# Rescheduling the combine weights of the second mixture, and the place of the low parts in an expert's first unit

## The chip, the cores and the metric

The kernel runs on one core of one Trainium2 chip. The metric is the device time of one execution in microseconds, the median of several runs; lower is better. A core has five engines with a queue of instructions each: TensorE (PE, matrix products), VectorE (DVE), ScalarE (ACT), GpSimd (POOL) and SyncE (SP, which here only issues DMA transfers). An engine works its queue in order, and an instruction waits on semaphores that other engines or transfers raise.

## The reference

Attention with a memory, then a soft mixture of experts, then a second mixture whose gates are balanced over rows and columns. The change touches the second mixture alone:

```python
def _moe_ref(x, phi, w1, w2):            # first mixture; its output is the second one's x
    ...
    return (c @ slot_out).astype(np.float32)      # c: 2304 x 32, slot_out: 32 x 512

def _moe2_ref(x, w_gate, w1, w2):
    N, D = x.shape                        # 2304, 512
    E = w_gate.shape[1]                   # 8 experts
    P = np.exp(logits - logits.max())     # logits = x @ w_gate
    for _ in range(8):
        P /= P.sum(1, keepdims=True) + 1e-09
        P /= P.sum(0, keepdims=True) + 1e-09
        P *= N / E
    for e in range(E):
        h = np.maximum(x @ w1[e], 0.0)    # 2304 x 1024
        ye = h @ w2[e]                    # 2304 x 512
        out += P[:, e:e + 1] * ye
```

## The kernel before, in words

Since x is `c @ slot_out`, with 32 slots, the first layer of expert e is `c @ (slot_out @ w1[e])`. The small product in brackets is formed by `prepare_a`, split by `split_a`, and copied into its place by 16 transfers (`move_a`, line 1077; sources `ahi` and `alo`). The weights c are multiplied by the gate P[:, e] beforehand, which is allowed because P is positive. So each expert needs its own turned combine weights: the tile `c4T`, whose 128 rows are four stacked copies of 32 slots, two of high parts and two of low parts (a float32 is split into a rounded part "h" and the rest "l", so that fast products keep the accuracy).

The 2304 tokens are nine units of 256. The 72 units (eight experts, nine units) run one after the other; a unit g has seven steps, k = 0 to 6. In step k TensorE makes one of seven products of the second layer (`product`, a scheme with seven instead of eight block products; the order is p5, p1, p7, p6, p2, p3, p4). Each product has 4 blocks f with three terms: high by high, high by low part of the weights (`wl`), low part of h by high: 12 matmuls with 256 columns. In step 1 TensorE also makes the first layer of the next unit (`layer1`, line 1097, 8 matmuls), so a unit has 92 matmuls. A unit of the first expert up to unit 4 is done in plain form (`plain`).

The weights of an expert are prepared during the units of the expert before: sums (line 996), high parts on ACT (line 999), low parts on POOL or DVE (line 1005). Those of the tiles BB1 and BB2 (named B11, T3, B21, B22 in the code) are overwritten in place, and their turn comes only in the last unit and the first one of the next expert, since the last unit still reads them.

The new combine weights for c4T come in two rounds, r = 0 for token tiles 0 to 8 and r = 1 for tiles 9 to 17: `part_c` (POOL: c by P[:, e]), `round_c` (ACT: high part), `rest_c` (POOL: low part), `blocks_c` twice (DVE: 32 by 32 blocks turned, z = 0 the high part, z = 1 the low part, into a tile `ct` of which there is one buffer), and `move_c` (SP: 16 transfers of 36 KB into c4T, line 1333). Before the change both rounds belong to units 5 and 6 of the expert before, and their transfers follow in units 5 and 7.

The order on PE, DVE, ACT and POOL is the order in which the loop at the end writes the instructions (`manual_schedule`); a table `side` says after which step the functions above are called: `beside(s, f)` puts f after step s = 7 g + k, `at(u, k, f)` is the same with unit and step apart. SP's order comes from the framework's scheduler and is shown below. With v = 9 (e - 1), units v to v + 8 are those of expert e - 1, and v + 9 is the first of expert e.

Of the kernel before, what the change touches and what calls it, by code (L numbers as in the profile page):

```python
# [21 lines left out]
def infini_attention_soft_moe_sinkhorn_moe(  # L22
# [15 lines left out]
    nc = tc.nc  # L38
    B, H, D, S = q.shape
# [72 lines left out]
    with ExitStack() as actx:  # L112
# [31 lines left out]
        for i in range(QTB):  # L144
            pr = []
            for nm, w in (("qz", 3 * TAIL), ("qx", 2 * TAIL)):
                t = e2.tile([P, w], F32R, name=f"{nm}{i}")
# [5 lines left out]
        for i in range(2):  # L153
            t = ep[i].tile([P, 2, S], F32R, name=f"klz{i}")
# [530 lines left out]
        def at(p, n, f, *args):  # L685

            fill.setdefault(3 * NT * p + n, []).append((f, args))
# [14 lines left out]
        for p in range(NP):  # L702
            b, hp = order[p]
# [68 lines left out]
    with bctx:  # L772
# [7 lines left out]
        for i in range(NBIG + 4, len(pieces)):  # L780

            k = i % (NBIG + 4 + NW)
# [140 lines left out]
    KH = KF // 2  # L923
# [401 lines left out]
            ct_[e, r, "t"][:, WR * z : WR * z + WR], cw[:, WR * (1 - z) : WR * (2 - z)]  # L1325
        )

    def move_c(e, r):
        ct = ct_[e, r, "t"]
        to = c4T[:, 0:N].bitcast(F32).rearrange("p (t j n) -> p t j n", j=4, n=32)  # L1330
        for z in range(4):
            for j in range(4):
                nc.sync.dma_start(  # L1333
                    to[32 * z : 32 * z + 32, NR * r : NR * r + NR, j],
                    ct[32 * j : 32 * j + 32, WR * (z // 2) : WR * (z // 2) + WR].rearrange(
                        "p (t n) -> p t n", n=32
                    ),
                )
# [3 lines left out]
    def beside(s, f, *args):  # L1342
        side.setdefault(s, []).append((f, args))
# [22 lines left out]
    def at(u, k, f, *args):  # L1366
        beside(7 * u + k, f, *args)

    def c_round(v, e, r, w):
        at(v, 1, part_c, e, r)  # L1370
        at(v, 2, round_c, e, r)
        at(v, 3, rest_c, e, r)
        at(v, 4, blocks_c, e, r, 0)
        at(v, 5, blocks_c, e, r, 1)
        at(w, 6, move_c, e, r)

    for k, u0, u1 in ((-1, 5, 7), (2, 7, 9)):
        for n, f in enumerate((scale_c, turn_c, store_c)):
# [1 line left out]
    s = 1  # L1380
# [9 lines left out]
        at(RAW - 1, 5 + i, w_lo, 0, "T3", i, "P")  # L1390
    for e in range(1, E):
        v = NU * (e - 1)
        c_round(v + 5, e, 0, v + 5)
        c_round(v + 6, e, 1, v + 7)
        at(v, 0, load_w1, e, e % 2)
        at(v + 3 * (e == 1), 4, load_raw, e)

        at(v + 1, 3 + 2 * (e == 1), prepare_a, e)
        at(v + 1, 4 + (e == 1), split_a, e)
        at(v + 1, 5 + (e == 1), move_a, e)  # L1400
        for i in range(2):
            for n, nm in enumerate(("T1", "T2", "T4")):

                s = 29 + 4 * (3 * i + n) if e == 1 else 7 * (v + 2 + 3 * i + n) + 1
                beside(s, w_sum, e, nm, i, "P")
                beside(s + 2 - (e == 1), w_hi, e, nm, i)
                beside(s + 3 - (e == 1), w_lo, e, nm, i, "P")
            at(v + 6 + i, 2, w_sum, e, "T3", i, "P")
        for nm, k in (("B11", 2), ("T3", 4), ("B21", 6), ("B22", 8)):
            for i in range(2):  # L1410
                at(v + 8, k + i, w_hi, e, nm, i)
                at(v + 8, k + i + (nm[0] == "B" and nm[1] == "2"), w_lo, e, nm, i, "D" if nm == "B22" and i else "P")
# [30 lines left out]
    def product(g, k):  # L1443
        e, u = units[g]
        a, b = PRODS[ORDER[k]]
        bank, half = PLACE[ORDER[k]]
        if (g, bank) not in Y:
            Y[g, bank] = ps_y.tile([P, DM], F32, tag="y", name=bank)
        o_ = Y[g, bank][:, CW * half : CW * half + CW]
        hh, hl = X[g, a, "h"], X[g, a, "l"]  # L1450
        wh, wl = W[e, b, "h"], W[e, b, "l"]
        for f in range(KH):
            nc.tensor.matmul(o_, hh[:, f, :], wh[:, f, :], start=f == 0, stop=False)  # L1453
            nc.tensor.matmul(o_, hh[:, f, :], wl[:, f, :], start=False, stop=False)  # L1454
            nc.tensor.matmul(o_, hl[:, f, :], wh[:, f, :], start=False, stop=f == KH - 1)  # L1455
        return o_

    def collect(g, k, y):
# [68 lines left out]
    with tc.manual_schedule(engines={E_.PE, E_.DVE, E_.Activation, E_.Pool}):  # L1527
# [27 lines left out]
        for g in range(len(units)):  # L1555
            nxt = g + 1 < len(units)
            for k in range(7):
                s = 7 * g + k
# [16 lines left out]
                else:  # L1575

                    EX[s + 1] = g, k, product(g, k)
                    if k == 1 and nxt:
                        layer1(g + 1)
# [74 lines left out]
```

## Time and profile before

| what | value |
|---|---|
| median of 3 runs (range) | 1141.69 us (1140.42 to 1143.72) |
| the profiled execution | 1150.51 us |
| its span in the trace, granted TensorE clock | 1148.4 us, 0.984 of full speed |
| busy: PE, DVE, POOL, ACT | 1091.0, 824.8, 680.7, 614.8 us |
| transfers into c4T (line 1333) | 224, 36 KB each, 2.0 us to landing |

The profiled execution is 8.8 us longer than the median of the plain runs. All times of single instructions below come from that execution. The second mixture begins at about 311 us, and its experts run from about 382 us to the end. "Busy" counts the time in which an engine works on at least one instruction; matmuls overlap, so a matmul that lasts 0.28 us in a row is followed by the next some 0.11 to 0.12 us after its own start.

### The profile page before, as it was taken

The page shows a single profiled execution, that of the slowest core. Times are in us where ns is not written, and L with a number is a line of the kernel's source. Part 1 is how long each engine was busy: PE and PEld are TensorE (multiplying, and loading weights), DVE is VectorE, ACT ScalarE, POOL GpSimd, SP SyncE. Part 2 cuts the span into 40 slices and gives each one's busy share as a digit, 9 for nine tenths or more (in the row PEclk, how much of TensorE's full clock was granted, in tenths as well). Part 3 has the DMA queues.
Part 4 walks back from the last instruction along what each step waited for, and adds up shares of the span by engine and source line. Part 5 has one row for each costly group of instructions (what it writes and reads, how often), then busy time and mean ns, then how long its engine had stood idle before and what let it go on. Part 6 is the DMA issues. An engine that isn't in the chain of part 4 may idle for free.

```text
span 1148.4 us, 24415 instructions
## 1 busy us (share of the span) xinstructions
PE 1091.0 (95%) x9103; PEld 990.2 (86%) x9103; DVE 824.8 (72%) x1839; ACT 614.8 (54%) x1301; POOL 680.7 (59%) x633
## 2 busy tenths in 40 slices
PE   6989998998999999999999999999999999999998
PEld 4767777773377899999899999999999999999998
DVE  7878888875167457777777777777777777777775
ACT  6788878761242656446344544544454454445442
POOL 4423333300153598688578767867776776788665
PEclk9999999997999999999999999999999999999999
DMA  6577677428922024014102501420150132011111
GB/s 152 161 219 223 193 217 219 106 105 354 383 88 74 1 41 149 19 22 132 57 1 32 158 19 20 119 71 1 30 160 19 17 97 92 5 27 24 54 51 55
DMA packets 110740, 113.97 MB, mean 99 GB/s; under 512 B 76320, under 2 KB 86688, under 8 KB 106528
## 3 DMA queue, kind: packets, MB, share of 16 engines
q1 hardware_dynamic: 110192, 112.34, 33.1%
q8 instruction: 72, 1.18, 0.4%
q14 instruction: 44, 0.36, 0.1%
q10 hardware_dynamic: 432, 0.09, 0.0%
HBM read 95.74 MB, written 4.72 MB: 87 GB/s over the span
## 4 chain that ended last, share of the span: by engine, by line
PE 67%; DVE 10%; POOL 5%; SPq 5%; ACT 5%; issue 4%; DMA 3%; DVEq 0%; ACTq 0%; POOLq 0%
PE y L1454 15%; PE y L1453 15%; PE y L1455 15%; PE l L1097 5%; SPq L1333 4%; PE po L447 3%; PE y L1420 3%; POOL BB2l L1005 2%; DMA kd<-in_k_dram 2%; PE pt L410 1%; PE ph L841 1%; DMA c4T<-ct 1%; PE pso L863 1%; ACT sm L371 1%; PE pa L1044 1%
## 5 line engine op out<-in xcount | busy, mean ns | idle before, releaser
L1121 DVE SCALAR_TENSOR_TENSOR f<-l,f 128x512 f32<-128x512 f32 x268 | 184.3, 688 | 89.5 <-ACT a11h L1127 70.8
L1138 POOL TENSOR_TENSOR s1l<-f,s1h 128x512 fp32r<-128x512 f32 x67 | 87.0, 1299 | 137.2 <-ACT s1h L1127 137.1
L1469 DVE TENSOR_TENSOR accA<-accA,y 128x512 f32<-128x512 f32 x125 | 85.5, 684 | 55.0 <-PE y L1455 54.0
L1117 ACT ACTIVATE f<-l 128x512 f32<-128x512 f32 x67 | 40.2, 599 | 138.7 <-PE l L1097 112.0
L1127 ACT ACTIVATE a12h<-l 128x512 fp32r<-128x512 f32 x72 | 43.2, 600 | 128.4 <-PE y L1455 88.0
L1138 POOL TENSOR_TENSOR s4l<-f,s4h 128x512 fp32r<-128x512 f32 x67 | 87.1, 1300 | 26.9 <-ACT s4h L1127 23.0
L1469 DVE TENSOR_TENSOR accB<-accB,y 128x512 f32<-128x512 f32 x125 | 85.1, 681 | 8.0
L1138 POOL TENSOR_TENSOR s3l<-f,s3h 128x512 fp32r<-128x512 f32 x67 | 87.0, 1298 | 2.0 <-ACT s3h L1127 2.0
L1138 POOL TENSOR_TENSOR s2l<-f,s2h 128x512 fp32r<-128x512 f32 x67 | 86.9, 1297 | 0.0
L1097 PE MATMUL l<-c4T,a 128*128 128x256 f32 x576 | 79.9, 282 | 4.3 <-DVE a22l L1134 4.3
L1454 PE MATMUL y<-BB2l,s4h 128*128 128x256 f32 x268 | 76.1, 284 | 6.4 <-POOL BB2l L1005 4.3
L1453 PE MATMUL y<-T1h,s1h 128*128 128x256 f32 x268 | 75.3, 281 | 4.8 <-DVE accA L1469 4.7
L371 ACT ACTIVATE sm<-sm,mn 128x128 f32<-128x128 f32 (+3 forms) x128 | 71.0, 556 | 15.9 <-DVE mn L367 14.6
L1005 POOL TENSOR_TENSOR BB1l<-raw,BB1h 128x512 fp32r<-128x512 f32 x32 | 41.5, 1311 | 62.6 <-ACT BB1h L999 62.6
L1097 PEld LDWEIGHTS l<-c4T,a 128*128 128x128 f32 x576 | 72.8, 189 | 6.1 <-DVE a22l L1134 5.7
L1454 PE MATMUL y<-BB2l,a12h 128*128 128x256 f32 x268 | 75.5, 282 | 0.3
L1453 PE MATMUL y<-BB2h,s4h 128*128 128x256 f32 x268 | 75.1, 280 | 0.7 <-ACT accD L1467 0.7
L1453 PE MATMUL y<-BB2h,a12h 128*128 128x256 f32 x268 | 75.5, 282 | 0.0
L1453 PE MATMUL y<-BB1h,a11h 128*128 128x256 f32 x268 | 75.3, 281 | 0.0
L1453 PE MATMUL y<-BB1h,s3h 128*128 128x256 f32 x268 | 75.3, 281 | 0.0
L1454 PE MATMUL y<-BB1l,s3h 128*128 128x256 f32 x268 | 75.3, 281 | 0.0
L1454 PE MATMUL y<-T4l,a22h 128*128 128x256 f32 x268 | 75.3, 281 | 0.0
(321 smaller groups left out, 4137.8 us busy)
## 6 DMA issues: line engine op xcount, KB each, us to landing
wm<-in_moe_w_dram SPq DMA_DIRECT2D x32, 1024.0 KB, 8.5
raw<-in_moe_w_dram SPq DMA_DIRECT2D x32, 512.0 KB, 4.4
w<-in_moe_w_dram SPq DMA_DIRECT2D x32, 512.0 KB, 5.1
qd<-in_q_dram SPq DMA_DIRECT2D x30, 288.0 KB, 4.2
kd<-in_k_dram SPq DMA_DIRECT2D x30, 288.0 KB, 4.7
c4T<-ct SPq DMA_DIRECT2D x224, 36.0 KB, 2.0
qp<-in_q_dram SPq DMA_DIRECT2D x15, 288.0 KB, 3.1
vt<-in_v_dram SPq DMA_DIRECT2D x16, 256.0 KB, 2.7
```

The lines of the kernel that those rows point to most:

```text
L371: nc.scalar.activation(out=sm[:, 0:n], in_=sm[:, 0:n], func=AF.Exp, scale=-1.0, bias=mnc, accum_out=X.sums[:, i, h : h + 1],)
L1005: eng(g).tensor_tensor(out=w_tile(e, nm, "l")[:, h], in0=full(e, nm, i), in1=w_tile(e, nm, "h")[:, h].bitcast(F32), op=ALU.subtract,)
L1097: nc.tensor.matmul(ph[:, f, :], a4s[e][:, P * (KH * j + f) : P * (KH * j + f) + P], c4T[:, UT * u : UT * u + UT], start=True, stop=True,)
L1117: nc.scalar.activation(out=f_tile(g, nm), in_=ph(g, nm), func=AF.Relu)
L1121: nc.vector.scalar_tensor_tensor(out=f_tile(g, nm), in0=ph(g, src), scalar=0.0, in1=b, op0=ALU.max, op1=op)
L1127: nc.scalar.activation(out=h_tile(g, nm, "h"), in_=ph(g, nm) if a else FU[g, nm], func=AF.Relu if a else AF.Copy)
L1138: nc.gpsimd.tensor_tensor(out=lo, in0=FU[g, nm], in1=hi, op=ALU.subtract)
L1333: nc.sync.dma_start(to[32 * z : 32 * z + 32, NR * r : NR * r + NR, j], ct[32 * j : 32 * j + 32, WR * (z // 2) : WR * (z // 2) + WR].rearrange(
L1453: nc.tensor.matmul(o_, hh[:, f, :], wh[:, f, :], start=f == 0, stop=False)
L1454: nc.tensor.matmul(o_, hh[:, f, :], wl[:, f, :], start=False, stop=False)
L1455: nc.tensor.matmul(o_, hl[:, f, :], wh[:, f, :], start=False, stop=f == KH - 1)
L1469: nc.vector.tensor_tensor(out=acc, in0=acc, in1=y, op=ALU.add)
```

## The change

Two edits.

First, `c_round` gets new places. Round 0 of expert e now starts after step 2 of the fifth unit (unit 4) of expert e - 1 (one unit later for e = 1), and round 1 only after step 1 of unit 1 of expert e itself. Inside a round the high part is turned right after it is made, and its 8 transfers (z = 0, 1) are issued two steps before the low part is made; the 8 transfers of the low part (z = 2, 3) follow four steps after the first 8. Tiles 9 to 17 of c4T, which round 1 writes, are first read by the first layer of unit 4, which is made in step 1 of unit 3.

Second, in the first unit of each expert but the first, the products with the weights B11, T3, B21 and B22 make their 4 terms with the low part of the weights last instead of in every block.

```diff
-    def move_c(e, r):
+    def move_c(e, r, zs):
...
-        for z in range(4):
+        for z in zs:
...
-    def c_round(v, e, r, w):
-        at(v, 1, part_c, e, r)
-        at(v, 2, round_c, e, r)
-        at(v, 3, rest_c, e, r)
-        at(v, 4, blocks_c, e, r, 0)
-        at(v, 5, blocks_c, e, r, 1)
-        at(w, 6, move_c, e, r)
+    def c_round(s, e, r):
+        for k, f, *a in (
+            (0, part_c), (1, round_c), (2, blocks_c, 0), (5, rest_c), (6, blocks_c, 1),
+        ):
+            beside(s + k, f, e, r, *a)
+        beside(s + 3, move_c, e, r, (0, 1))
+        beside(s + 7, move_c, e, r, (2, 3))
...
-        c_round(v + 5, e, 0, v + 5)
-        c_round(v + 6, e, 1, v + 7)
+        c_round(7 * (v + 4 + (e == 1)) + 2, e, 0)
+        c_round(7 * (v + 10) + 1, e, 1)
...
-        for f in range(KH):
-            nc.tensor.matmul(o_, hh[:, f, :], wh[:, f, :], start=f == 0, stop=False)
-            nc.tensor.matmul(o_, hh[:, f, :], wl[:, f, :], start=False, stop=False)
-            nc.tensor.matmul(o_, hl[:, f, :], wh[:, f, :], start=False, stop=f == KH - 1)
+        terms = ((hh, wh), (hh, wl), (hl, wh))
+        seq = [(f, t) for f in range(KH) for t in terms]
+        if u == 0 and e and (b[0] == "B" or b == "T3"):
+            seq = [(f, t) for f in range(KH) for t in terms[::2]] + [(f, terms[1]) for f in range(KH)]
+        for n, (f, (a, b)) in enumerate(seq):
+            nc.tensor.matmul(o_, a[:, f, :], b[:, f, :], start=n == 0, stop=n == 3 * KH - 1)
```

SP's queue from the loads of expert 7's weights (`raw`, written in the first unit of expert 6) to the transfers behind `move_a` (`a`), before:

```order
L955 DMA raw_12910<-in_moe_w_dram 128x1024
L955 DMA raw_12912<-in_moe_w_dram 128x1024
L955 DMA raw_12914<-in_moe_w_dram 128x1024
L955 DMA raw_12916<-in_moe_w_dram 128x1024
L1077 DMA a_13082<-ahi 32x256 x4
L1077 DMA a_13082<-alo 32x256 x4
L1077 DMA a_13082<-ahi 32x256 x4
L1077 DMA a_13082<-alo 32x256 x4
L1333 DMA c4T<-ct 32x9x32 x32
```

The same place of SP's queue now:

```order
L955 DMA raw_12887<-in_moe_w_dram 128x1024
L955 DMA raw_12889<-in_moe_w_dram 128x1024
L955 DMA raw_12891<-in_moe_w_dram 128x1024
L955 DMA raw_12893<-in_moe_w_dram 128x1024
L1333 DMA c4T<-ct 32x9x32 x8
L1077 DMA a_13072<-ahi 32x256 x4
L1077 DMA a_13072<-alo 32x256 x4
L1077 DMA a_13072<-ahi 32x256 x4
L1077 DMA a_13072<-alo 32x256 x4
L1333 DMA c4T<-ct 32x9x32 x24
```

The 32 transfers that stood behind `move_a` were both rounds of expert 7. Now the first half of expert 6's round 1 stands ahead of `move_a`'s 16, and its second half behind them, followed by the 16 of expert 7's round 0.

DVE's queue in unit 6 of expert 6, where both halves of round 1 (`ct`) stood among the sums (`accA`, `accB`) that free the product banks `y`, before:

```order
L1134 SCALAR_TENSOR_TENSOR a11l<-l_13791,a11h 128x512
L1324 STREAM_TRANSPOSE ct<-cw 128x288
L1469 TENSOR_TENSOR accA<-accA,y_13822 128x512
L1121 SCALAR_TENSOR_TENSOR f<-l_13786,f 128x512
L1324 STREAM_TRANSPOSE ct<-cw 128x288
L1469 TENSOR_TENSOR accB<-accB,y_13800 128x512
```

The first half of expert 6's round 1 now, in unit 1 of that expert (`alo` is the split behind `prepare_a`):

```order
L1471 TENSOR_TENSOR accD<-accD,y_12980 128x256
L1324 STREAM_TRANSPOSE ct<-cw 128x288
L1121 SCALAR_TENSOR_TENSOR f<-l_12967,f 128x512
L1134 SCALAR_TENSOR_TENSOR a11l<-l_12972,a11h 128x512
L1055 TENSOR_TENSOR alo<-pa,ahi 128x256
L1471 TENSOR_TENSOR accA<-accA,y_13001 128x512
```

The transposes left unit 6's chain of sums; the first of them now runs before `alo`, so its transfers come ahead of `move_a`.

PE's queue in the first unit of expert 7 at the change from product p2 (`a12`) to p3 (`s4`), before:

```order
L1454 MATMUL y_14292<-BB2l,a12h 128x256
L1455 MATMUL y_14292<-BB2h,a12l 128x256
L1453 MATMUL y_14270<-BB2h,s4h 128x256
L1454 MATMUL y_14270<-BB2l,s4h 128x256
L1455 MATMUL y_14270<-BB2h,s4l 128x256
```

The end of p3 there now:

```order
L1457 MATMUL y_14247<-BB2h,s4h 128x256
L1457 MATMUL y_14247<-BB2h,s4l 128x256
L1457 MATMUL y_14247<-BB2l,s4h 128x256 x4
L1457 MATMUL y_14330<-T4h,a22h 128x256
L1457 MATMUL y_14330<-T4l,a22h 128x256
```

The low part BB2l was first read by the second matmul of the product, and is now first read by the ninth.

## Rows read from the trace of the kernel before

**Rows 1.** The page, parts 1 and 4: busy shares, and the chain by engine.
```profile
PE 1091.0 (95%) x9103; PEld 990.2 (86%) x9103; DVE 824.8 (72%) x1839; ACT 614.8 (54%) x1301; POOL 680.7 (59%) x633
PE 67%; DVE 10%; POOL 5%; SPq 5%; ACT 5%; issue 4%; DMA 3%; DVEq 0%; ACTq 0%; POOLq 0%
```
**Rows 2.** Waits of PE, whole span: total us, times, longest.
```profile
PE y L1453 <- DVE accA L1469: 4.7, 5, 1.4
PE y L1454 <- POOL BB2l L1005: 4.3, 6, 0.7
PE l L1097 <- DVE a22l L1134: 4.3, 7, 2.1
PE y L1454 <- DVE BB2l L1005: 2.0, 1, 2.0
```
**Rows 3.** Waits of all engines, whole span: DVE's on the transfers.
```profile
DVE ct L1324 <- DMA c4T<-ct: 17.8, 7, 3.5
```
**Rows 4.** Chain of waits in time: start us, us, what; layer1 and prepare_a.
```profile
456.10 1.86 PE pa L1044 x32
464.98 0.91 PE l L1097 x8
475.41 0.91 PE l L1097 x8
...
893.54 0.94 PE l L1097 x8
...
904.38 0.94 PE l L1097 x8
...
928.11 1.20 PE l L1097 x8
938.83 0.91 PE l L1097 x8
...
961.03 0.91 PE l L1097 x8
964.66 1.86 PE pa L1044 x32
...
984.63 0.94 PE l L1097 x8
```
**Rows 5.** Timeline of PE, 905 to 956: matmuls after a wait (in brackets).
```profile
924.63 0.36 PE L1453 MATMUL y<-T1h,s1h 128*128 128x256 f32 x1 [1.41 <-DVE accA L1469]
...
928.11 1.20 PE L1097 MATMUL l<-c4T,a 128*128 128x256 f32 x8 [0.36 <-DVE a22l L1134]
...
955.41 0.39 PE L1454 MATMUL y<-BB2l,s4h 128*128 128x256 f32 x1 [0.71 <-POOL BB2l L1005]
```
**Rows 6.** Chain of waits, 860 to 965: first and last of 16 transfers.
```profile
909.58 0.63 SPq L1333
...
919.47 3.65 DMA c4T<-ct
923.44 0.48 DVE ct L1324
```
**Rows 7.** Timeline of SP, 940 to 1045: first and last quarter of move_a.
```profile
967.00 2.47 SPq L1077 DMA_DIRECT2D a<-ahi  x4
...
974.59 2.49 SPq L1077 DMA_DIRECT2D a<-alo  x4
```
**Rows 8.** Timeline of DVE, 956 to 988: the sum in unit 1 of expert 6.
```profile
964.17 0.41 DVE L1469 TENSOR_TENSOR accD<-accD,y 128x256 f32<-128x256 f32 x1
```
**Rows 9.** The page, part 6: KB each, us from issue to landing.
```profile
c4T<-ct SPq DMA_DIRECT2D x224, 36.0 KB, 2.0
```
**Rows 10.** Timelines of POOL and DVE in a first unit: low parts of BB2.
```profile
951.11 4.25 POOL L1005 TENSOR_TENSOR BB2l<-raw,BB2h 128x512 fp32r<-128x512 f32 x3
...
544.66 4.75 DVE L1005 TENSOR_TENSOR BB2l<-raw,BB2h 128x512 fp32r<-128x512 f32 x1
```
**Rows 11.** Stretch behind the DVE wait: us, busy (x) by engine, PEclk, DMA share, GB/s.
```profile
549.50:552.50 3.00, 3.00 (x14) 3.00 (x15) 2.90 (x5) 1.23 (x3) 1.28 (x1) 0.50 0.51 175
```

## Prediction

> **What bounds the kernel now.** I read the page first: TensorE is busy 95% of the span and holds 67% of the chain that ended last [rows 1]. So only what makes PE wait, or what changes its pace, can move the time. The second view is PE's own waits [rows 2]. Those that the change can touch are of two kinds. On DVE's sums (`accA`, 5 waits, 4.7 us) and on `a22l` (7 waits, 4.3 us, of which the longest, 2.1, lies ahead of expert 1 and has another cause); and on the low parts `BB2l` (6 waits on POOL, 4.3 us; one on DVE, 2.0).
>
> The third view tells what stands behind the first kind: DVE waits 17.8 us in 7 places for transfers out of `ct` [rows 3]. In the chain, 16 transfers of round 0 are issued from 909.58 to 919.47, the last lands 3.65 us later, and only then does DVE turn round 1 into the same buffer, at 923.44 [rows 6]. Sums queue behind that transpose, and PE stands still 1.41 us at 924.63 and 0.36 at 928.11 [rows 5]. The second kind: at 955.41 PE waits 0.71 us for BB2l [rows 5], which ends POOL's run of three at 951.11 + 4.25 = 955.36 [rows 10].
>
> The fourth view is the spacing of the first layers in the chain, one per unit [rows 4]. It gives a **pace**, and there are two of them: 475.41 - 464.98 = 10.43 us a unit, and 904.38 - 893.54 = 10.84. With 92 matmuls a unit that is 113.4 and 117.8 ns per matmul. The trace keeps one pace over many units and changes it at a wait or at `prepare_a`: slow at 904.38, fast after the waits at 924 to 928, and slow again behind the `prepare_a` at 964.66 (the first layers at 893.54 and 904.38 stand in the same part of the expert before). I know no cause; a microsecond of fast time is worth 10.84 / 10.43 - 1 = 0.039 us. Fast time in an expert is at present about 928.11 to 964.66, 36.6 us, or 256 us in seven.
>
> **The change part by part**, against the profiled execution of 1150.5 us (8.8 above the median; I carry the difference over to the median).
>
> *A. The rounds apart.* The transpose no longer finds `ct` in use, since the other round lies half an expert away, so the DVE wait and the PE waits behind it go. What they cost: from 904.38 to 928.11 are 23.73 us for two slow units of 10.84, so 2.05 lost, and from 928.11 to 938.83 are 10.72 for a fast unit of 10.43, 0.29 lost; together 2.34 for 1.77 us of idle time, so a restart costs 0.29 beside the wait. Idle 4.7 + 2.2, and 11 restarts: 6.9 + 3.2 = 10.1 us. What is late next there: nothing that I see, since PE runs through units 2 to 5 without a wait. The moved POOL pieces (28 of each kind) keep their number, and POOL is busy 59% of the span [rows 1]. **-10.1.**
>
> *B. Low parts last.* From 938.83 to 961.03 are 22.20 us for two fast units, 20.86: 1.34 lost per boundary, 7 boundaries, 9.4 us (the 4.75 us of the DVE piece in one of them [rows 10] I take for a single event, and leave it). With the new order BB2l is wanted at the ninth matmul of p3. From 938.83 that matmul is 92 + 8 + 36 + 8 = 144 starts away: 955.16 at the fast pace, 0.2 before POOL is done, so 0.2 + 0.29 stay; at the slow pace 955.79, and nothing stays. The matmuls are as many as before. I take seven tenths of 7 x 0.5 as remaining: 9.4 - 2.5. **-6.9** (ends -5.9 and -9.4).
>
> *C. Round 1 behind `move_a`.* This is a new wait. In unit 1 of expert 6 DVE ends its sum at 964.17 + 0.41 [rows 8]; the transpose takes 0.48 [rows 6], so SP can begin at about 965.1. The 16 transfers of a round start every (919.47 - 909.58) / 15 = 0.66 us [rows 6], so the first 8 hold SP for 5.3 us, to 970.4. Then come `move_a`'s 16, which held SP from 967.00 to 977.08 [rows 7]: 10.1 us, to 980.5. The last of the other 8 starts 7 x 0.66 later, at 985.1, and lands 2.0 us after its issue [rows 9]: 987.1. `layer1` of unit 4, the first reader of tiles 9 to 17, is due at 984.63 [rows 4]. PE waits 2.5 us and pays 0.29 for the restart; the products behind it wait in PE's queue, and all other engines wait for them. Experts 1 to 6 have this; for 7 there is no `move_a`. In expert 1 the pace is fast and the due time earlier by (984.63 - 964.66) - (475.41 - 456.10) = 0.66. Sum: 6 x 2.8 + 0.7 = **+17.4**. Ends: 3.65 us to landing as in [rows 6] instead of 2.0 adds 1.65 each, +27; an SP that passes the transfers at a third less would leave none of it, 0, which is a rival below.
>
> The Trainium skill, "DMA: Bandwidth & Descriptors", section "Rules for kernel authors", says to issue a transfer early, compute, and wait late, so that its fixed cost is overlapped. By that rule alone C is 0, as the second half is written some 11 us before its reader. The rows speak against it here: the fixed cost would be hidden, SP's 24 issues ahead of the last transfers are not.
>
> *D. The clock after a longer wait.* After PE's one wait of 2.0 us the granted clock was 0.50 from 549.5 to 552.5, and 14 matmuls ran where 25 fit at the slow pace [rows 11]: 11 x 0.118 = 1.3 us. After the 1.41 us at 924.63 the full pace went on. The new waits of 2.5 us lie above both, on one sighting; I take the drop for three of six: **+3.9** (ends 0 and 7.8).
>
> *E. The pace.* The wait in unit 3 restarts PE, and I expect the pace to be mostly fast afterwards, as behind 928.11. From 987 to the next `prepare_a` (an expert lasts 9 units and 1.9 us of it, some 102 us) are 79 us for experts 1 to 5, and for 6 it is 161 to the end: 556 us that could be fast. With three quarters of it fast, an estimate, 417 against 256: 161 x 0.039 = **-6.3** (ends: all fast -11.7, all slow +10.0).
>
> Sum: -10.1 - 6.9 + 17.4 + 3.9 - 6.3 = -2.0. On the median: **1139.7 us**. So I expect two gains of 17 us to be all but eaten by one new wait.
>
> **The rivals.**
> *The second half lands in time.* Then C and D vanish, no wait restarts PE, and the slow pace that follows `prepare_a` stays: -10.1 - 9.4 + 10.0 = -9.5, 1132.2 us. For it: only the low end of C. The rule of the Trainium skill above would have it so. Against it: SP's spacing in [rows 6] and [rows 7], which lets nothing overtake.
> *Slower: the restart falls into the slow pace.* Place: `layer1` in unit 3. Price: E is +10.0 instead of -6.3, B is complete: -10.1 - 9.4 + 17.4 + 3.9 + 10.0 = +11.8, 1153.5 us. It decides from the point at which fast time is no more than the present 256 us, since the sum without E is already +4.3. For it: after `prepare_a` and at the end of the span the slow pace holds for long; against it the restart at 928.11.
> *All restarts fast, the clock never drops.* -10.1 - 5.9 + 17.4 - 11.7 = -10.3, 1131.4 us. For it the 1.41 us wait that left the clock alone; against it [rows 11].
>
> **How the numbers follow.** The forecast, with its own range 1134 to 1146 us (E and D between half and whole), gets 0.45; the half in time 0.17; the slow restart 0.20; all fast 0.18. The range from 1129 to 1150 leaves out the far end of the slow case and a little of the fast ones. About 0.3% (3.4 us) is what a measurement can tell from no change. Faster by more: 0.16 of the half in time, 0.17 of all fast, 0.17 of the forecast (3.4 lies close above its 2.0), 0.50. Slower: 0.19 of the slow case and 0.04 of the forecast, 0.23. The rest, 0.27, is no change.
>
> **What would show it.** A: DVE's wait of `ct` on the transfers gone, no wait of PE on `accA` at unit 7. B: waits on BB2l gone or under 0.3 us. C: six waits of PE's `layer1` on the c4T transfers of 2 to 3.5 us, and in SP's timeline 8, 16 and 8 issues without a gap; if these waits are absent, C is wrong and the first rival holds. D: a granted clock of a half behind them. E: distances of 10.43 or 10.84 us between first layers from unit 3 on. Wrong altogether would be a PE that waits in units 4 to 8 for POOL or ACT, which does not occur there at present [rows 2].

## The result, and the profile after

The changed kernel takes 1156.33 us (median of 4 runs, 1155.05 to 1159.27) against 1142.7 us (median of 4, 1140.42 to 1146.91): a ratio of 1.0119, 95% interval 1.0082 to 1.0155. It is slower by 1.2%; 1139.7 was predicted, with a range from 1129 to 1150. (Ratios, here and below, leave out runs more than 1.5% above the fastest one of their kernel, which matters for e4, where five of twelve go.) The profiled execution took 1156.27 us, span 1154.5, against 1150.5 and 1148.4 before.

The page of the changed kernel, parts 1 and 4, answers to [rows 1]:

```profile
PE 1086.4 (94%) x9103; PEld 989.3 (86%) x9103; DVE 823.0 (71%) x1839; ACT 615.5 (53%) x1301; POOL 681.2 (59%) x633
PE 73%; DVE 9%; POOL 5%; ACT 4%; DMA 4%; issue 4%; SPq 2%; DVEq 0%; ACTq 0%; POOLq 0%
```

The instructions are as many as before. PE is busy 4.6 us less and the span is 6.1 us longer, so the time went into waits. PE's waits (total us, times, longest), to be read beside [rows 2]:

```profile
PE l L1097 <- DMA c4T<-ct: 23.0, 6, 4.1
...
PE y L1457 <- POOL BB2l L1005: 1.4, 5, 0.3
```

The waits on `accA` at unit 7 are gone (4.7 us), those on POOL's BB2l are down from 4.3 to 1.4, the one of 2.0 on DVE's is gone, and `a22l` keeps only the wait ahead of expert 1 (2.1). Among DVE's waits the one of `ct` on the transfers [rows 3] is absent too. In their place stand six waits of `layer1` on c4T. SP's timeline in expert 6 (start us, us, what) shows where they come from:

```profile
972.24 5.75 SPq L1333 DMA_DIRECT2D c4T<-ct  x8
978.10 2.46 SPq L1077 DMA_DIRECT2D a<-ahi  x4
980.65 2.43 SPq L1077 DMA_DIRECT2D a<-alo  x4
983.13 2.50 SPq L1077 DMA_DIRECT2D a<-ahi  x4
985.67 2.71 SPq L1077 DMA_DIRECT2D a<-alo  x4
988.49 5.54 SPq L1333 DMA_DIRECT2D c4T<-ct  x8
```

8, 16 and 8 issues with almost no gap: the last one begins 21.2 us after the first. The chain of waits in time of the same place, with first layers and `prepare_a` (start us, us, what), answers to [rows 4] and [rows 6]:

```profile
971.91 1.86 PE pa L1044 x32
...
993.41 1.98 DMA c4T<-ct
995.39 0.35 issue
995.73 1.66 PE l L1097 x8
...
1008.04 0.91 PE l L1097 x8
...
1018.47 0.91 PE l L1097 x8
```

The last transfer's issue begins at 993.41; it has landed 1.98 us later, and PE starts 0.35 us after that. `prepare_a` to the first layer of unit 4 took 984.63 - 964.66 = 19.97 us before [rows 4]; here it is 995.73 - 971.91 = 23.82: a loss of 3.85 us. Then the unit behind the wait lasts 1008.04 - 995.73 = 12.31 us where the next one lasts 10.43.

PE's timeline has all six waits (start us, us of eight matmuls, and in brackets the wait):

```profile
477.33 2.01 PE L1097 MATMUL l<-c4T,a 128*128 128x256 f32 x8 [4.06 <-DMA c4T<-ct]
...
580.51 2.04 PE L1097 MATMUL l<-c4T,a 128*128 128x256 f32 x8 [3.89 <-DMA c4T<-ct]
...
684.60 1.21 PE L1097 MATMUL l<-c4T,a 128*128 128x256 f32 x8 [3.55 <-DMA c4T<-ct]
...
787.39 1.55 PE L1097 MATMUL l<-c4T,a 128*128 128x256 f32 x8 [4.06 <-DMA c4T<-ct]
...
892.18 1.18 PE L1097 MATMUL l<-c4T,a 128*128 128x256 f32 x8 [3.55 <-DMA c4T<-ct]
...
995.73 1.66 PE L1097 MATMUL l<-c4T,a 128*128 128x256 f32 x8 [3.86 <-DMA c4T<-ct]
```

Two stretches behind such waits, after that at 995.73 and after that at 892.18 (columns as in [rows 11]: us, busy and number by engine, granted clock, DMA share, GB/s):

```profile
996.40:999.60 3.20, 3.20 (x17) 3.20 (x17) 1.38 (x2) 1.95 (x4) 0.04 (x1) 0.50 0.00 0
892.20:895.20 3.00, 3.00 (x25) 3.00 (x26) 0.93 (x2) 1.39 (x3) 0.00 (x0) 1.00 0.00 0
```

PE is busy in all of both. In the first the granted clock is 0.50, the lower of the two levels (1.2 of 2.4 GHz), and only 17 matmuls fall in 3.2 us; in the second it is full, with 25 in 3.0 us. The distances between first layers give the price of each wait's aftermath: 12.30, 13.55, 12.30, 12.61, 11.08 and 12.31 us for the unit behind the wait, against 10.43 at the fast pace (first, second, third, sixth) or 10.84 at the slow (fourth, fifth): 1.87, 3.12, 1.87, 1.77, 0.24 and 1.88 lost. Five of six fell to half; the second lost twice.

### The profile page after: what moved, and what is told of

Its sections match the earlier page's. It is cut to its first block, busy times and chain, and to the rows that moved or that the text cites. A ratio compares the mean times of both kernels' runs of the same rounds, so it can differ in the third digit from the quotient of the medians.

```text
span 1154.5 us, 24445 instructions
## 1 busy us (share of the span) xinstructions
PE 1086.4 (94%) x9103; PEld 989.3 (86%) x9103; DVE 823.0 (71%) x1839; ACT 615.5 (53%) x1301; POOL 681.2 (59%) x633
## 3 DMA queue, kind: packets, MB, share of 16 engines
q8 instruction: 72, 1.18, 0.4%
## 4 chain that ended last, share of the span: by engine, by line
PE 73%; DVE 9%; POOL 5%; ACT 4%; DMA 4%; issue 4%; SPq 2%; DVEq 0%; ACTq 0%; POOLq 0%
PE y L1457 50%; PE l L1097 6%; PE po L447 3%; PE y L1420 3%; SPq L1333 2%; POOL BB2l L1005 2%; PE ph L841 1%; DVE sm L367 1%; PE pa L1044 1%; PE pt L410 1%; ACT sm L371 1%; DMA w<-in_moe_w_dram 1%; DMA c4T<-ct 1%; DMA kd<-in_k_dram 1%; DVE ot L511 1%
## 5 line engine op out<-in xcount | busy, mean ns | idle before, releaser
L1457 PE MATMUL y<-BB1h,s3h 128*128 128x256 f32 x268 | 76.5, 289 | 0.0
L1457 PE MATMUL y<-BB1h,s3l 128*128 128x256 f32 x268 | 76.3, 289 | 0.0
L1457 PE MATMUL y<-T2h,s2h 128*128 128x256 f32 x268 | 75.2, 281 | 0.0
L1457 PE MATMUL y<-T2l,s2h 128*128 128x256 f32 x268 | 75.0, 280 | 0.0
L1457 PE MATMUL y<-T2h,s2l 128*128 128x256 f32 x268 | 74.8, 279 | 0.0
L1457 PE MATMUL y<-T4h,a22h 128*128 128x256 f32 x268 | 74.4, 278 | 0.0
L1457 PE MATMUL y<-T1h,s1h 128*128 128x256 f32 x268 | 74.4, 278 | 0.0
L1457 PE MATMUL y<-T1l,s1h 128*128 128x256 f32 x268 | 74.4, 278 | 0.0
L1457 PE MATMUL y<-T1h,s1l 128*128 128x256 f32 x268 | 74.4, 278 | 0.0
```

The source lines that it names most:

```text
L1457: nc.tensor.matmul(o_, a[:, f, :], b[:, f, :], start=n == 0, stop=n == 3 * KH - 1)
```

## The experiments

Each compares a kernel with runs of the kernel before on the same chip. "Fast time" below is worked out from the trace of each profiled run: the distances between neighbouring 256-column products after 380 us, added up where they are nearer to 113.4 than to 117.8 ns. Before has 251 us of it, the changed kernel 452.

**e1, the second edit alone** (the kernel before, with the changed order of the sums, L1452 to L1457).

```diff
+        if u == 0 and e and (b[0] == "B" or b == "T3"):
+            seq = [(f, t) for f in range(KH) for t in terms[::2]] + [(f, terms[1]) for f in range(KH)]
```

> The kernel before with only the second edit (low parts last in an expert's first unit). Theory (the changed kernel is slower because layer1 of unit 4 waits for round 1's second half, six times 3.5 to 4.1 us, with the clock halved behind most of them): this kernel has no such wait, the waits on BB2l shrink from 0.7 to 0.3 us or less, 3 to 8 us faster than before, ratio 0.993 to 0.997. Rival (the new order of the matmuls is what costs): 8 us or more slower, ratio above 1.007. Rival (a restart's pace decides, not the waits): anything from 0.990 to 1.010, with the fast time in the trace telling which.

Measured 1142.15 us, ratio 0.9976 (0.9944 to 1.0008). PE's waits:

```profile
PE y L1457 <- DVE accA L1471: 5.9, 5, 1.7
...
PE y L1457 <- DVE BB2l L1005: 5.0, 2, 2.5
...
PE y L1457 <- POOL BB2l L1005: 1.4, 5, 0.3
```

The wait on POOL shrinks as in the changed kernel, from 4.3 to 1.4. Less arrives in the time than expected: the waits on accA and on DVE's own piece of BB2l, which the edit doesn't touch, were longer in this run (5.9 for 4.7, two of 2.5 for one of 2.0). So the edit does its part, but its gain alone can't be told from none.

**e2, the first edit alone** (c_round and move_c changed, sums in the old order).

```diff
-        c_round(v + 5, e, 0, v + 5)
-        c_round(v + 6, e, 1, v + 7)
+        c_round(7 * (v + 4 + (e == 1)) + 2, e, 0)
+        c_round(7 * (v + 10) + 1, e, 1)
```

> The kernel before with only the first edit (both rounds moved, sent in halves). Theory: the six waits of layer1 on the c4T transfers stay, 3.5 to 4.1 us each, and the waits on BB2l come back to 0.7: slower than before by 16 to 22 us, ratio 1.014 to 1.019. Rival (the matmul order costs): as fast as before or faster, ratio 0.985 to 1.000.

Measured 1166.86 us, ratio 1.0195 (1.0151 to 1.0239): slower than with both edits, and just above the 1.014 to 1.019 that were expected.

```profile
PE l L1097 <- DMA c4T<-ct: 21.7, 6, 4.3
...
PE y L1454 <- POOL BB2l L1005: 4.1, 6, 0.7
```

The loss belongs to this edit. The clock fell behind all six waits, three times for twice as long as otherwise, where the changed kernel has this once; and with the old sums the waits on BB2l stay.

**e3, `move_a` one unit later** in the changed kernel, so that it no longer stands between the two halves of round 1 (expert 1 unchanged: its `move_a` comes at the end of its unit).

```diff
-        at(v + 1, 5 + (e == 1), move_a, e)
+        at(v + 1 + (e > 1), 6 if e == 1 else 2, move_a, e)
```

> The changed kernel with move_a called one unit later (behind the second half of round 1), so that SP issues 10 transfers instead of 24 ahead of that half's last one. Nothing else is moved; a4 is needed only six units later. Theory: the six waits of 23.0 us in all and the five clock drops go, the rest stays: 25 to 32 us faster than the changed kernel, that is 1124 to 1132 us, ratio to before 0.984 to 0.991; if no restart is left the slow pace holds for longer, and 1134 us is the upper end. Rival (the pace of the restart is the cause, or the rounds' new places on POOL and DVE): no better than 1148 us, ratio 1.005 or more.

Measured 1131.74 us, ratio 0.9888 (0.9857 to 0.992), as expected. SP's timeline in expert 6:

```profile
952.58 5.87 SPq L1333 DMA_DIRECT2D c4T<-ct  x8
958.55 1.20 SPq L1077 DMA_DIRECT2D a<-ahi  x2
960.31 5.22 SPq L1333 DMA_DIRECT2D c4T<-ct  x8
965.58 1.25 SPq L1077 DMA_DIRECT2D a<-ahi  x2
```

The last c4T issue is over 13.0 us after the first one began instead of 21.8, no wait on c4T is left in the whole trace, and the kernel is 2.3% faster than the changed one, by their ratios to before. The cause of the slowdown is the queue on SP, and nothing else of the change. This is the proof of step C's place.

**e5, a dose between**: the changed kernel with 12 of `move_a`'s 16 transfers ahead of the second half and 4 behind it.

```diff
-        at(v + 1, 5 + (e == 1), move_a, e)
+            at(v + 1, 5, move_a, e, (0, 1, 2))
+            at(v + 2, 2, move_a, e, (3,))
```

> The changed kernel with a quarter of move_a (4 of 16 transfers) called behind round 1's second half instead of ahead of it. Theory (SP's issue time sets the wait): the wait of layer1 shrinks by 4 x 0.63 = 2.5 us, from 3.5 to 4.1 down to 1.0 to 1.6 us, six times; such waits leave the clock at its full level. Against the changed kernel 6 x 2.5 = 15 us less waiting and 9 us less at half clock, fast time about as long: some 1132 us, ratio to before 0.985 to 0.994. Rival (the drops come from anything else than the length of the wait): the drops stay, 1141 us, ratio 0.996 to 1.000. Rival (the second half's place matters, not SP's queue): the waits stay as they are, ratio 1.010.

Measured 1141.88 us, ratio 0.9949 (0.992 to 0.9978); the interval touches both the theory's 0.985 to 0.994 and the rival's 0.996 to 1.000 and decides nothing. The waits do. PE's timeline:

```profile
478.38 1.18 PE L1097 MATMUL l<-c4T,a 128*128 128x256 f32 x8 [0.81 <-DMA c4T<-ct]
578.69 1.16 PE L1097 MATMUL l<-c4T,a 128*128 128x256 f32 x8 [1.17 <-DVE accA L1475]
677.42 1.16 PE L1097 MATMUL l<-c4T,a 128*128 128x256 f32 x8 [1.08 <-DVE accA L1475]
779.52 1.18 PE L1097 MATMUL l<-c4T,a 128*128 128x256 f32 x8 [1.98 <-DMA c4T<-ct]
879.95 1.17 PE L1097 MATMUL l<-c4T,a 128*128 128x256 f32 x8 [0.74 <-DVE accA L1475]
979.67 2.05 PE L1097 MATMUL l<-c4T,a 128*128 128x256 f32 x8 [2.59 <-DMA c4T<-ct]
```

8.4 us of waits instead of 23.0, and only the longest was followed by half clock: its eight matmuls took 2.05 us, the others 1.16 to 1.18. Four issues fewer ahead are 4 x 0.65 = 2.6 us, and the waits fell by (23.0 - 8.4) / 6 = 2.4 each. (Three of them the profile lays to `accA`, whose sum ended 0.02 to 0.44 us before PE started. But in all three the last c4T transfer landed 0.20 us before the start, as it did in the waits at 478.38 and 779.52, and a first layer reads c4T; so I count them with the others.)

**e4, the rounds apart without the halves**: the kernel before, with round 1 one unit later.

```diff
-        c_round(v + 6, e, 1, v + 7)
+        c_round(v + 7, e, 1, v + 7)
```

> The kernel before with round 1's four pieces on POOL, ACT and DVE called one unit later (unit 7 instead of 6), its transfers where they were: DVE no longer meets the transfers of round 0 in ct, and nothing is put between move_a and its readers. It takes the first kind of wait alone (term A). Theory: DVE's 17.8 us of waits and PE's waits on accA go, 6 to 10 us faster than before, ratio 0.991 to 0.995; if the fast pace that followed those waits is lost with them, half of it comes back: 0.996 to 1.000.

Measured 1134.92 us, ratio 0.9883 (0.9844 to 0.9921). The waits on accA and of `ct` on the transfers are gone, as step A says. The medians of all runs, 1145.63 and 1134.92, lie 10.7 us apart, about A's 10.1. The profiled runs differ by more, 15.7 us, since fast time was 479 us instead of 251, which nothing in the edit asks for.

**e6, e4 with the second edit.**

```diff
-        c_round(v + 6, e, 1, v + 7)
+        c_round(v + 7, e, 1, v + 7)
...
+            seq = [(f, t) for f in range(KH) for t in terms[::2]] + [(f, terms[1]) for f in range(KH)]
```

> Round 1 one unit later as in the run before (transfers where they always were) together with the low parts last. Theory: the gains of the two add up, since they lie at different places: 0.988 times 0.998 to 0.993, that is a ratio of 0.981 to 0.987 to before. If each gain was only a luckier pace, they don't add: 0.986 to 0.995.

Measured 1141.46 us, ratio 0.9931 (0.9895 to 0.9967): the two gains don't add. PE had next to no waits left (2.0 us on DVE's BB2l once, 0.2 on POOL), and the slow pace, 10.84 us a unit, went on through whole experts: fast time 146 us. What the waits gave back, the pace took.

**e7, e3 with the sums in the old order.**

```diff
-        terms = ((hh, wh), (hh, wl), (hl, wh))
-        seq = [(f, t) for f in range(KH) for t in terms]
...
+            nc.tensor.matmul(o_, hh[:, f, :], wl[:, f, :], start=False, stop=False)
```

> The kernel with move_a one unit later, with the second edit undone (low parts in every block again). Theory: the waits on BB2l come back, 0.4 to 0.7 us and 0.29 for the restart at 7 boundaries, 5 to 7 us slower than with the edit, ratio to before 0.992 to 0.996. Rival (the second edit does nothing here): ratio 0.988 as with it.

Measured 1137.68 us, ratio 0.9923 (0.9892 to 0.9955), at the near end of what was expected. Beside e3's 0.9888 the second edit is worth some 0.3 to 0.4%, but the intervals overlap. Between e2 and the changed kernel the difference is 0.8% (1.0195 to 1.0119), of which the two more long drops of the clock in e2 are a part.

**e8, e3 with all of BB2's low parts on POOL**, against the long DVE piece described below.

```diff
-                at(v + 8, k + i + (nm[0] == "B" and nm[1] == "2"), w_lo, e, nm, i, "D" if nm == "B22" and i else "P")
+                at(v + 8, k + i + (nm[0] == "B" and nm[1] == "2"), w_lo, e, nm, i, "P")
```

> The kernel with move_a one unit later, with the last low part of BB2 on POOL instead of DVE. In several traces this one DVE piece lasted 4.75 to 5.2 us instead of 1.05 to 1.5 and ended only when POOL had nothing to do. Theory (DVE waits for POOL at the SBUF side): no such piece is left, no half clock behind it; but POOL's four pieces end 1.25 us later, so PE waits about 0.6 us at 7 boundaries: between 3 us faster and 5 us slower than with DVE, ratio to before 0.986 to 0.993.

Measured 1139.8 us, ratio 0.9954 (0.9929 to 0.9979): a miss, slower than e3.

```profile
PE y L1457 <- POOL BB2l L1005: 10.6, 7, 1.9
```

DVE's long pieces are gone, but POOL, with a fourth piece, is 1.5 us late at each of seven boundaries, which costs more than one event of 2.5 us.

**e9, e3 with a short product of 128 columns behind `prepare_a`, waiting for `split_a`** (it writes a part of `pa` that nothing reads): a small wait, to restart PE there on purpose.

```diff
+        nc.tensor.matmul(G["pa", e][:, 256:384], src[:, 0:128], src[:, 0:128], start=True, stop=True)
...
+        at(v + 1, 3 + 2 * (e == 1), restart_pe, e, True)
```

> The kernel with move_a one unit later, with one more product of 128 columns after each prepare_a, into a part of its bank that nothing reads, which waits for the split behind prepare_a: PE stands still about 1 us there and starts anew, six times. Theory on the pace (a wait that ends at PE draws the pace anew, mostly the fast one, while prepare_a alone mostly leaves the slow one): fast time rises from 207 us to 350 us or more; waits cost 6 x 1.3 = 8 us, the fast time gives back 6 to 12: ratio to before 0.983 to 0.991. Rival (the pace has nothing to do with restarts): fast time as without, 8 us slower, ratio 0.996.

Measured 1137.27 us, ratio 0.9957 (0.9924 to 0.999). The waits came out as meant:

```profile
PE pa L1076 <- DVE alo L1055: 6.8, 7, 1.0
```

Fast time rose from 207 to 422 us as expected, but the time missed: 215 x 0.039 = 8.4 us of pace are spent on 6.8 us of waits and their restarts, and a second long DVE piece came on top (4.5 us for 2.5).

**e10, the same product without the wait**: it reads an old BB1h tile and stands ahead of `split_a`.

```diff
+        src = a2s[e][0] if late else BB[1, "h"][:, 0, 0]
...
+        at(v + 1, 3 + 2 * (e == 1), restart_pe, e, False)
```

> The control for the run before: the same extra product at the same place, but it waits for nothing (it reads an old weight tile and stands ahead of the split). Theory: fast time stays near 200 us, ratio 0.987 to 0.992. Rival (any extra instruction there changes the pace): fast time 350 us or more, ratio 0.978 to 0.984.

Measured 1115.83 us (4 runs, 1111.93 to 1116.02), ratio 0.976 (0.9727 to 0.9793). The theory, that it takes a wait to change the pace, fell, and its rival held, the ratio even lying below its range: a product without a wait does it too (`split_a` stands one slot earlier as well, as in e9; the two weren't tried apart). Chains of e3 and of e10 in expert 6, `prepare_a` and first layers:

```profile
952.25 1.86 PE pa L1044 x32
...
961.37 0.94 PE l L1097 x8
...
972.21 0.94 PE l L1097 x8
```

```profile
937.86 1.86 PE pa L1044 x32
939.72 0.26 PE pa L1076
...
946.85 0.91 PE l L1102 x8
...
957.28 0.91 PE l L1102 x8
```

10.84 us a unit in e3 and 10.43 in e10, where the pace is the fast one behind all six `prepare_a` from expert 1 on: fast time 667 us. It beats the kernel before and the changed one. The terms add up: 460 us more fast time x 0.039 = 17.9, e3's DVE event of 2.5 + 0.3 + 1.3 = 4.1 us away, less seven products of 0.26 (1.8) and some 3 us for small waits on BB2l with their restarts: 17. The profiled runs differ by 1132.89 - 1115.90 = 17.0.

**e11, e3 once more**, the same kernel without any edit, on the chip of e10.

> The kernel with move_a one unit later once more, beside the two others, for a second trace of its pace and a firmer ratio: 0.986 to 0.992, no wait of layer1 on the c4T transfers, fast time between 100 and 350 us.

Measured 1125.3 us, ratio 0.9843 (0.9806 to 0.988), a little faster than expected. Fast time in its profiled run of 1118.34 us was 484 us, beyond the expected 350, in e3's of 1132.89 us 207: one kernel, two paces behind the same `prepare_a` (fast behind four of six, against one). So the kernel's text does not fix the pace, and the difference is worth 277 x 0.039 = 10.8 us. As e3 ran on another chip, that it changes from execution to execution on one chip isn't shown.

**e12, the extra product in the kernel before**, with nothing of the change.

```diff
+        nc.tensor.matmul(G["pa", e][:, 256:384], src[:, 0:128], src[:, 0:128], start=True, stop=True)
...
-        at(v + 1, 4 + (e == 1), split_a, e)
+        at(v + 1, 3 + 2 * (e == 1), restart_pe, e, False)
+        at(v + 1, 3 + 2 * (e == 1), split_a, e)
```

> The kernel before, with nothing of the change, but with the extra 128-column product ahead of split_a of e10 (it adds a product whose result nothing reads, and sets split_a one slot earlier). Theory, that the product alone turns the pace behind prepare_a to fast: fast time after 380 us of 550 us or more against 251 to 350 in kernels without it, the waits on accA and BB2l stay, as in rows 2, ratio 0.982 to 0.991. Rival, that e10's pace came from the product together with a PE that waits for nothing: fast time 250 to 400 us, ratio 0.995 to 1.001.

Measured 1139.49 us, ratio 0.9945 (0.9921 to 0.9968). Fast time was 623 us, as the theory wanted (the kernels without the product have 146 to 484, not the 251 to 350 that I named); the ratio was not.

```profile
PE y L1459 <- DVE accA L1475: 6.2, 6, 1.3
...
PE y L1460 <- DVE BB2l L1005: 4.0, 2, 2.0
```

The pace should give 372 x 0.039 = 14.5 us. The products cost 1.8, and the waits were longer by 3.5 (accA 1.5, DVE's BB2l 2.0, with a half clock of 1.3 behind the second one): some 8 remain, and the profiled runs differ by 1150.51 - 1142.34 = 8.2. So pace and waits are two separate accounts, and e10 is good because it has both.

## Why the prediction was wrong

The mechanism was seen and the sizes weren't: the new wait came where C puts it, but C and D priced it too low, by 12.4 us together, and the step from the profiled execution to the median failed besides. Against the profiled executions the sum should have been -2.0 and was 1156.27 - 1150.51 = +5.8. Step by step:

- **A, right.** The waits named are gone in the changed kernel and in e4. In e4 the pace moved too, so its 10.1 us come out only by subtraction: of the 15.7 between the profiled runs 228 x 0.039 = 8.9 are pace, and a second long DVE piece cost e4 2.1 + 0.3 + 1.3 = 3.7 that before did not pay, which leaves 15.7 - 8.9 + 3.7 = 10.5.
- **B, right in kind, somewhat smaller.** 531.34 to 552.77 in the changed kernel's chain is 21.43 us for two fast units, so 0.57 remains of 1.34 at a fast boundary (0.5 predicted), and at the slow one before 968.27 nothing (957.44 to 968.27 is 10.83). But the 9.4 counted seven boundaries, and at one of them PE waited not for POOL but for the long DVE piece, which is listed below by itself. For six boundaries it is 8.0, and 1.4 + 5 x 0.29 = 2.9 remain: 5.2 gone where 6.9 were predicted.
- **C, the step that failed first, in its size.** 2.5 us a wait were predicted; 23.0 / 6 = 3.8 measured. The working for expert 6: SP began 0.33 us after `prepare_a` started (0.44 predicted), needed 21.17 us from its first issue to the start of the last one (20.0 predicted: the first 8 took 5.86, not 5.3, `move_a`'s 16 took 10.39, not 10.1, and the next seven 4.92, not 4.6), the landing took 1.98 (2.0), and PE started 0.35 after it (0 predicted). That last term was in sight: in [rows 6] the landing at 919.47 + 3.65 = 923.12 releases an instruction at 923.44. Together 2.5 - 0.1 + 1.2 + 0.3 = 3.9. With six restarts: +24.7 instead of +17.4.
- **D, too small, for the same reason.** Waits of 3.5 to 4.1 us took the clock down five times of six, by 1.87 - 0.29 = 1.6 each and 2.8 once: 10.75 - 6 x 0.29 = +9.0 instead of +3.9. It wasn't independent of C: e5's six waits, up to 2.59 us, brought one drop. A term whose size depends on another's should have been priced with it over the whole range. It also went by one sighting where the trace has two: PE waited 2.07 us ahead of expert 1 as well, and the granted clock was 0.50 from 395.5 to 398.5. The length alone doesn't decide: behind two waits of 2.49 us on BB2l in e5 (448.5 to 451.5 and 749.0 to 752.0) it stayed at 1.00.
- **E, right, by a guess.** 452 us of fast time (417 predicted): (452 - 251) x 0.039 = -7.8 for -6.3. Behind four waits of six the fast pace followed, each time until about the next `prepare_a` or to the end. That three quarters would be fast was an estimate without a cause; it came out near.
- **Left out**: before's one long DVE piece with its wait of PE, restart and half clock, which I took for a single event and left in. It doesn't occur in the changed kernel: 2.0 + 0.3 + 1.3 = -3.6.

-10.1 - 5.2 + 24.7 + 9.0 - 7.8 - 3.6 = +7.0, where the profiled runs show +5.8; the terms account for it to within 1.2 us. So of the 16.6 us between 1139.7 and 1156.3, 5.8 + 2.0 = 7.8 come from the terms. The other 8.8 come from **the last step, carrying the profiled execution's excess over to the median**. Before's profiled run lay 8.8 us above its median; that of the changed kernel lies on it. Other kernels show that one execution can lie so far off: the profiled runs of e1 and e7 are 7.1 and 5.8 us above their medians, that of e11 is 7.0 below. What before's excess was made of isn't shown, since there is a single trace of before; the pace could be it, as e3 and e11 differ by 10.8 us of it.

The rivals: the half in time is refuted by SP's timeline. With it falls the rule of the Trainium skill ("DMA: Bandwidth & Descriptors", section "Rules for kernel authors") read as a price: the half was written early and awaited late, and still 23.0 us were lost. In expert 6 PE stood ready at 995.73 - 3.86 = 991.87, and SP began the last issue only 1.54 us later; so the 1.98 us to landing, which the rule would hide, lay open too. The slow restart had nearly the right time, 1153.5, for a wrong reason: fast time rose. The clock that never drops is refuted by the five drops.

**Open** is what sets the pace. Shown: it holds over many units, it differs between traces of one kernel (e3, e11), `prepare_a` turns it over to the other one (last section), and with a product of 128 columns behind `prepare_a`, and `split_a` a slot earlier, it is fast there whatever it was ahead (e10, e12). Of the 60 `prepare_a` of experts 1 to 6 in before, the changed kernel and e1 to e8, 15 left the fast pace behind them, and those are the ones that PE reached at the slow pace. Not shown: why `prepare_a` does so, and what decides the pace between one of them and the next.

## What to carry to other kernels

A write that is moved ahead of its reader is only as early as its place in the issuing queue: count the issues ahead of its last transfer, with their spacing from the trace (here 0.62 to 0.73 us each), add the landing and the release, and compare with the reader's due time; if the margin is negative, move the other traffic behind it (e3). Price a new wait on the bounding engine with what comes after it, restart and half clock (here up to 3.1 us on top of a wait of 3.9), over the whole range of the wait. And before a difference of 1% is predicted from one trace, look whether that trace stands at its median: an excess of one execution need not pass to the next kernel.

## What the hardware showed that I hadn't expected

**`prepare_a` turns the pace of PE over, and with one small product behind it the pace comes out fast.** In the eleven traces without the extra product the pace behind each `prepare_a` of experts 1 to 6 was the other one than ahead of it, 66 times of 66: 47 times 113.4 ns a matmul ahead and 117.8 behind, 19 times the other way. One of the 19, in e3 (PE's timeline, the first and the last of 24 matmuls ahead of the `prepare_a` at 652.81, and of 24 behind it):

```profile
649.89 0.28 PE L1457 MATMUL y<-BB1h,s3h 128*128 128x256 f32 x1
...
652.60 0.28 PE L1457 MATMUL y<-T2h,s2l 128*128 128x256 f32 x1
...
657.50 0.28 PE L1457 MATMUL y<-T4h,a22h 128*128 128x256 f32 x1
...
660.11 0.28 PE L1457 MATMUL y<-T1h,s1l 128*128 128x256 f32 x1
```

23 distances take 2.71 us ahead, 117.8 ns each, and 2.61 us behind, 113.5; the granted clock is 1.00 in both. With 7 products of 128 columns, 0.26 us each, the pace was fast behind all twelve such `prepare_a` of e10 and e12, five of which PE reached at the slow pace and seven at the fast, and fast time was 667 and 623 us where 207 and 251 were. In e9, whose product waits, it was fast behind four of six. Since `split_a` moved along in all three, that the product does it alone isn't shown.

**A DVE piece can starve beside POOL.** The same piece, low parts of BB2 on DVE, 128x512, takes 1.0 to 1.5 us in most boundaries and 4.75 to 5.2 in a few. The changed kernel, then e3, POOL and DVE (start us, us, what):

```profile
958.89 4.25 POOL L1005 TENSOR_TENSOR BB2l<-raw,BB2h 128x512 fp32r<-128x512 f32 x3
...
960.95 1.03 DVE L1005 TENSOR_TENSOR BB2l<-raw,BB2h 128x512 fp32r<-128x512 f32 x1
```

```profile
736.57 3.84 POOL L1005 TENSOR_TENSOR BB2l<-raw,BB2h 128x512 fp32r<-128x512 f32 x3
...
741.57 1.29 POOL L1138 TENSOR_TENSOR s2l<-f,s2h 128x512 fp32r<-128x512 f32 x1
...
738.23 5.18 DVE L1005 TENSOR_TENSOR BB2l<-raw,BB2h 128x512 fp32r<-128x512 f32 x1
```

In the first, POOL's three pieces take 4.25 us, 0.41 more than in the second, and DVE is through in 1.03. In the second POOL works through five instructions without a gap, and DVE's piece ends at 743.41, 0.55 us after POOL went idle at 742.86. In before's event it is 549.41 [rows 10] after 548.86, again 0.55, as in all 20 such events of the traces. The Trainium skill, "SBUF — State Buffer", section "SBUF: two separate sides", says that a DVE instruction with two inputs in SBUF and a GpSimd instruction that reads SBUF compete for a shared pair of ports, which the one that starts first holds for its whole instruction while the other is blocked. The rows agree with one being held up; but here DVE was held up over several instructions of POOL in a row, 5.18 us against 1.03. That the port is the cause isn't shown by these runs. The event came one to four times in before, e1 to e7, e9, e11 and e12, and not in the changed kernel and e10. In e8, which takes the piece from DVE, there is none either.
